# Forward step of a recurrent attention kernel: mask products, a V cast, two postponed projections and a copy are reordered

## The chip, the core and the metric

The kernel runs on one core of a Trainium2 chip. Its engines work in parallel, each through its own instructions in order: TensorE (PE, matrix products; PEld is its loading of weights), VectorE (DVE), ScalarE (ACT), GpSimd (POOL) and SyncE (SP), which here only issues DMAs. PE writes to PSUM, the others copy from there to SBUF. Sixteen DMA engines move data between SBUF and the chip's memory and within SBUF; SP's DMAs go out on one hardware queue, POOL's on a software queue. The metric is the device time of one execution in microseconds (us). Kernels are compared by the median of several executions; a profile is one further execution.

## The reference

It is one training step (forward and gradients) of a layer of recurrent attention with a small memory, followed by a SwiGLU layer. The change is in the forward of the attention alone:

```python
mem = mem0                                   # 8 rows
for s in range(n_seg):                       # 64 segments of 32 rows, D = 448
    xs = x[:, s * seg_len:(s + 1) * seg_len, :]
    h = jnp.concatenate([mem, xs], axis=1)   # 40 rows
    q = jnp.einsum('btd,dhe->bhte', h, Wq)   # 16 heads of 256
    k = jnp.einsum('btd,dhe->bhte', h, Wk)
    v = jnp.einsum('btd,dhe->bhte', h, Wv)
    scores = jnp.einsum('bhqe,bhke->bhqk', q, k) * scale
    scores = jnp.where(mask[None, None], scores, -1000000000.0)
    p = softmax(scores)
    o = jnp.einsum('bhqk,bhke->bhqe', p, v)
    o = jnp.einsum('bhte,hed->btd', o, Wo)
    mem = o[:, :M, :]                        # the next segment needs these 8 rows
    outs.append(o[:, M:, :])
```

The eight output rows that become the next segment's memory make the segments a chain.

## The kernel before

The program has five stages one after another: the load of inputs and weights with the first layer norm, the forward chain over 64 segments, the SwiGLU layer with its gradients, the backward chain over the segments, and the weight gradients. Within an engine the order of the instructions is the order in which the Python code calls them (a manual schedule); waits between engines follow from the tiles that are read and written. DMAs on SP's queue take eight completion semaphores in turn, so that a DMA is issued only when the one eight before it has landed.

**One step** (forward_chain, the loop over s; t, r = divmod(s, 4)) works on 32 of a segment's 40 rows: the memory's 8 rows and 24 of its own. The other 8 rows of each segment depend on no memory, so they are handled for four segments at once, in pieces between the steps ("postponed" work, below).

1. K, then Q is projected (proj, L471), each in two halves of 512 columns. The four row groups of PE work at once, so that a projection lies in PSUM as four groups of 32 partitions. DVE and ACT cast the halves to Kev and Qev.
2. tr_half (L485) turns them by products with a unit matrix, four blocks of 128x128 per half; DVE and ACT copy them into kT and qT. POOL puts the postponed rows of kB and qB into the same tiles (L719, L720).
3. The first half of V is projected (L479); the scores of eight heads of each half are accumulated into two PSUM tiles s_ps (L516); then the second half of V.
4. Softmax of each half: maximum and difference on DVE (L759, L761), the exponential on ACT (L763), sum, reciprocal and product on DVE (L770, L772, L773). The mask is not added there: mask_mm (L498) has put it into s_ps beforehand by a product of a unit matrix and a mask tile, two products for each half (partitions 0 to 39 and 64 to 103).
5. The casts of V (Vev) must be moved to other partitions to form V_sb: v_shift (L667, L437), of the second half two groups by DMA on SP (D_) and two by DVE (V). v_b_rows (L663) adds the postponed rows of V by four DMAs on SP.
6. P is turned by PE (p_turn, L783), copied by p_ev into PT, and multiplied with V_sb (L816), first for one half of the heads, then for the other. The outputs oA and oB are evacuated by DVE and ACT.
7. The output projection (wo_mm, L600) leaves four partial sums of each token on four partition groups. They are copied to part (L434), transposed back by two products (turn, L524), and added by gsum (L529) into hA, the next step's memory rows. This ends the chain of a step.

K, Q and P are also stored for the backward stage: KtokA, QtokA (L766, L767) and Vtok (L802) by SP, P_all (L799) by POOL.

**Postponed pieces.** In the steps r = 1, 2, 3 of a tile t, the K, Q and V rows of the next tile that need no memory are projected (b_units, "k", "q", "v"); in r = 0 the output projection of the previous tile's such rows (o_units). Each unit is cut into pieces that the step calls at fixed places: u1 and its cast e1 after the softmax, u2 between P's two turnings, u3 (8 products of 512 columns) between the two halves of the product with V, its cast e3 after gsum. One step later (`late`) ut turns the cast rows by eight products (L583) between the output projection and turn, and one more step later (`late2`) et copies them on ACT into kB or qB. So K's rows are turned in the step r = 2 and Q's in r = 3, and both are needed in the next r = 0.

Of the kernel before, what the change touches and what calls it, by code (L numbers as in the profile page):

```python
# [10 lines left out]
BF16 = mybir.dt.bfloat16  # L11
# [4 lines left out]
P = 128  # L16
# [166 lines left out]
def run_all(k: _K):  # L183
# [89 lines left out]
    with tc.tile_pool(name="wfwd", bufs=1) as wf, \  # L273
# [14 lines left out]
        nc.gpsimd.affine_select(out=maskf[:], in_=maskf[:], compare_op=ALU.is_ge, fill=-1e9 / k.scale,  # L288
                                base=0, pattern=[[-1, L]], channel_multiplier=1)
        nc.gpsimd.memset(maskf[0:M, :], 0.0)  # L290
        maskr = wf.tile([L, H // 2 * L], BF16)
        for hh in range(H // 2):
            nc.vector.tensor_copy(out=maskr[:, hh * L:(hh + 1) * L], in_=maskf[:])
        k.part = wf.tile([P, DP], FP32, name="part")
        k.partB = wf.tile([P, DP], FP32, name="partB")
        nc.vector.memset(k.part[:], 0.0)
# [110 lines left out]
def forward_chain(k: _K, hA, NWIN, Wq_sb, Wk_sb, Wv_sb, Wo_sb, maskr, work, stage, ff):  # L407
# [17 lines left out]
    def ps1(dtype=FP32):  # L425
        if dtype == FP32:
            return k.pspool.tile([P, 512], FP32, tag="ps", name="psf")
        return k.pspool.tile([P, 1024], BF16, tag="ps", name="psh")

    def V(out, in_):  # L430
        nc.vector.tensor_copy(out=out, in_=in_)

    def A(out, in_):
        nc.scalar.copy(out=out, in_=in_)  # L434
# [47 lines left out]
    def tr_half(ev, half):  # L482
        pt = ps1(BF16)
        for j in range(4):
            nc.tensor.transpose(pt[:, j * P:(j + 1) * P], ev[:, half * HB + j * P:half * HB + (j + 1) * P], ident[:, :])  # L485
        return pt[:, 0:HB].rearrange("p (j g t) -> p j g t", j=4, g=G)

    def fm_view(dst, half, t0, t1):
        return dst[:].rearrange("p (g j) n -> p j g n", g=G)[:, 4 * half:4 * half + 4, :, t0:t1]
# [5 lines left out]
    S_v = [x[0:NR, 0:HQ * L].rearrange("p (h n) -> p h n", n=L) for x in S_ps]  # L495

    def mask_mm(half):
        for gg in range(2):  # L498
            nc.tensor.matmul(S_ps[half][QB * gg:QB * gg + L, 0:HQ * L], lhsT=ident[0:L, 0:L], rhs=maskr[:, 0:HQ * L],
                             start=True, stop=False, skip_group_check=True)  # L500

    def hpos(hh):
        return (hh // 4) * 2 + hh % 2
# [34 lines left out]

    tiles = {}

    def b_units(t, which):
        W_sb = {"k": Wk_sb, "q": Wq_sb, "v": Wv_sb}[which]
        T = tiles[t]
        st = {}

        def stat(kc):
            return T.hB[0:DB, kc, :, :]

        def mm(ps, half, kcs=range(4)):
            if which == "v":  # L550
                proj_v(ps, stat, half, kcs)
            else:
                proj(ps, W_sb, stat, half, kcs)

        def u1():
            st["p0"] = ps1(FP32)
            mm(st["p0"], 0)

        def e1():
            tg = "bevv" if which == "v" else "bev"  # L560
            st["ev"] = stage.tile([P, GF], BF16, name=tg, tag=tg, bufs=2)
            A(st["ev"][:, 0:HB], st["p0"][:, :])

        def u2():
            st["p1"] = ps1(FP32)
            mm(st["p1"], 1, range(0, 2))

        def u3():
            mm(st["p1"], 1, range(2, 4))

        def e3():
            V(st["ev"][:, HB:GF], st["p1"][:, :])
            if which == "v":
                T.vB = st["ev"]
            else:
                nc.gpsimd.dma_start(out=dr["KtokB" if which == "k" else "QtokB"][t], in_=st["ev"][:])

        def ut():
            if which == "v":
                return  # L580
            pt = ps1(BF16)
            for j in range(NJ):
                nc.tensor.transpose(pt[:, j * P:(j + 1) * P], st["ev"][:, j * P:(j + 1) * P], ident[:, :])  # L583
            st["pt"] = [pt[:, half * HB:(half + 1) * HB].rearrange("p (j g t) -> p j g t", j=4, g=G) for half in range(2)]

        def et():
            if which == "v":
                return
            dst = stage.tile([P, MC, SEG], BF16, name=which + "B", tag=which + "B", bufs=2)
            for half in range(2):  # L590
                A(fm_view(dst, half, 0, SEG), st["pt"][half])
            setattr(T, which + "B", dst)
        return dict(u1=u1, e1=e1, u2=u2, u3=u3, e3=e3, ut=ut, et=et)

    partB = k.partB

# [6 lines left out]
    def o_units(t):  # L603
        T = tiles[t]
        st = {}

        def mm(i0, i1):
            for i in range(i0, i1):
                for c in range(4 * i, 4 * i + 4):
                    wo_mm(st["pO"], T.oB[:, c, :], c, c % 2, c < 2, c >= MC - 2)  # L610

        def u1():
            st["pO"] = ps1(FP32)
            mm(0, 4)

        def e1():
            pass

        def u2():
            mm(4, 6)  # L620

        def u3():
            mm(6, 8)

        def e3():
            A(partB[:, 0:2 * DB], st["pO"][:, 0:2 * DB])

        def ut():
            st["y"] = turn(partB)

        def et():
            for kc in range(KC):
                gsum(T.aT[0:DB, kc, :].rearrange("p (r j) -> p r j", r=4)[:, :, XA:SEG],
                     st["y"][:, kc, :, :].rearrange("p (r i) g -> p r i g", r=4))
        return dict(u1=u1, e1=e1, u2=u2, u3=u3, e3=e3, ut=ut, et=et)

    def none_units():
        def f():
            pass
        return dict(u1=f, e1=f, u2=f, u3=f, e3=f, ut=f, et=f)  # L640

    def out_pe(t):
        T = tiles[t]
# [25 lines left out]
    def v_shift(V_sb, Vev, half, gs, eng):  # L669
        for g in gs:  # L670
            gg, g2 = divmod(g, 2)
            o = V_sb[QB * gg:QB * gg + SEG, g2 * GF + half * HB:g2 * GF + (half + 1) * HB]
            eng(o, Vev[32 * g:32 * g + 32, half * HB:(half + 1) * HB])
# [5 lines left out]
    pend = []  # L679
    for w in "kqv":  # L680
        u = b_units(0, w)
        for n in ("u1", "e1", "u2", "u3", "e3", "ut", "et"):
            u[n]()
    V_sb = work.tile([P, 2 * GF], BF16, name="V_sb", bufs=1)
    nc.gpsimd.memset(V_sb[:], 0.0)
# [1 line left out]
    for i in range(2):  # L687
# [1 line left out]
        nc.gpsimd.memset(Ps[i][:], 0.0)  # L689
        PTs.append(work.tile([P, 2, 4, 2 * L], BF16, name=f"PT{i}", bufs=1))  # L690
        nc.gpsimd.memset(PTs[i][:], 0.0)
    mask_mm(0)
    mask_mm(1)
    late = none_units()
    late2 = none_units()

    for s in range(NSEG):
# [40 lines left out]
        V(fm_view(kT, 0, 0, SEG), tr_half(Kev, 0))  # L738
        A(fm_view(kT, 1, 0, SEG), tr_half(Kev, 1))
        V(fm_view(qT, 0, 0, SEG), tr_half(Qev, 0))  # L740
        V(fm_view(qT, 1, 0, SEG), tr_half(Qev, 1))
        if s == NSEG - 1:
            ff.load_first()
# [13 lines left out]
        for half in range(2):  # L757
# [3 lines left out]
            nc.vector.tensor_tensor(out=S_sb[half][0:NR], in0=S_v[half],  # L761
                                    in1=mx[half][0:NR].unsqueeze(2).to_broadcast([NR, HQ, L]), op=ALU.subtract)
            nc.scalar.activation(out=E_sb[0:NR, half], in_=S_sb[half][0:NR], func=ACT.Exp, scale=k.scale)  # L763
        A(Vev[:, HB:GF], pv1[:, :])
        v_shift(V_sb, Vev, 1, (0, 1), D_)
        nc.sync.dma_start(out=dr["KtokA"][s], in_=Kev[:])  # L766
        nc.sync.dma_start(out=dr["QtokA"][s], in_=Qev[:])  # L767
        for half in range(2):
# [3 lines left out]
            nc.vector.reciprocal(out=rs[half][0:NR], in_=ssum[half][0:NR])  # L772
            nc.vector.tensor_tensor(out=hsel(P_sb, half), in0=hview(E_sb[0:NR, half]),  # L773
                                    in1=hview(rs[half][0:NR].unsqueeze(2).to_broadcast([NR, HQ, L])), op=ALU.mult)
        v_shift(V_sb, Vev, 1, (2, 3), V)
        cur["u1"]()
        cur["e1"]()
        PT = PTs[s % 2]
        ppt = [ps1(BF16), ps1(BF16)]

# [4 lines left out]
        def p_ev(half, e, eng):  # L785
            eng(PT[QB * e:QB * e + L, half, :, e * L:(e + 1) * L].rearrange("p (g a) n -> p g a n", g=2),
                ppt[half][QB * e:QB * e + L, 0:2 * P].rearrange("p (a g n) -> p g a n", a=2, g=2)[:, :, :, 0:L])

        if s + 1 < NSEG:
            mask_mm(0)  # L790
            mask_mm(1)
        p_turn(0)
        p_ev(0, 0, A)
        p_ev(0, 1, A)
        cur["u2"]()
        p_turn(1)
        p_ev(1, 0, A)
# [2 lines left out]

        for gg in range(2):
            nc.sync.dma_start(out=dr["Vtok"][s, gg], in_=V_sb[QB * gg:QB * gg + 48, :])  # L802

        oAv = T.oA[:].rearrange("p (g j) n -> p g j n", g=G)
        oBv = T.oB[:].rearrange("p (g j) n -> p g j n", g=G)
        obs = []
        for half in range(2):
            if half == 1:
                cur["u3"]()
            for gg in range(2):  # L810
                po = ps1()
                pw = po[:, 0:8 * L].rearrange("p (a e c n) -> p a e c n", a=2, e=2, c=DC)
                for i in range(2):
                    for dc in range(DC):
                        c0 = gg * GF + half * HB + i * Dh + dc * P
                        nc.tensor.matmul(pw[:, i, :, dc, :], lhsT=V_sb[0:NR, c0:c0 + P],  # L816
                                         rhs=PT[0:NR, half, 2 * gg + i, :].rearrange("p (e n) -> p e n", e=2),
                                         start=True, stop=True)
                pov = po[:, 0:8 * L].rearrange("p (g j n) -> p g j n", g=2, j=4)
                eng = V if gg == 0 else A  # L820
                eng(oAv[:, 2 * gg:2 * gg + 2, 4 * half:4 * half + 4, r * SEG:(r + 1) * SEG], pov[:, :, :, 0:SEG])
                obs.append((eng, oBv[:, 2 * gg:2 * gg + 2, 4 * half:4 * half + 4, r * M:(r + 1) * M], pov[:, :, :, SEG:L]))
# [6 lines left out]
        for i in range(MC):  # L829
            c = order[i]  # L830
            wo_mm(pO, T.oA[:, c, r * SEG:(r + 1) * SEG], c, i % 2, i < 2, i >= MC - 2)
        A(part[:, 0:2 * DB], pO[:, 0:2 * DB])
        late["ut"]()
        if r == 0 and t + 1 < NT:
            xl = xl_next
            ppx = prep_pe(xl)
# [1006 lines left out]
```

## Time and profile before

| | us |
|---|---|
| runs, median of 3 | 3031.98 (3018.99 to 3051.59) |
| profiled execution | 3044.81, its span 3043.0 |

Sums of stretches of the profiled execution (busy us):

| stretch, us | what | PE | PEld | DVE | ACT | POOL | clock |
|---|---|---|---|---|---|---|---|
| 0 to 66.8 | loads, first rows | 14.59 | 5.84 | 22.04 | 8.53 | 10.91 | 0.78 |
| 66.8 to 975 | forward chain | 857.83 | 497.37 | 532.69 | 422.48 | 212.22 | 0.99 |
| 975 to 1345 | SwiGLU and its gradients | 341.97 | 179.97 | 255.79 | 204.63 | 78.08 | 0.96 |
| 1345 to 2350 | backward chain | 906.40 | 515.85 | 563.06 | 452.34 | 245.38 | 0.97 |
| 2350 to 3043 | weight gradients | 654.95 | 331.13 | 128.32 | 76.33 | 190.66 | 0.98 |

Groups of the forward chain that the change touches (mean duration of one):

| line | what | count | ns |
|---|---|---|---|
| L499 PE | mask product, 40x160 | 256 | 242 (median) |
| L583 PE | turning of postponed K, Q, 128x128 | 256 | 219 (median) |
| L434 ACT | cast of V, 128x512 | 124 | 576 |
| L434 ACT | copy into kB, qB, 128x512 | 60 | 589 |
| L434 ACT | copy of the sums, part, 128x224 | 64 | 345 |
| L431 DVE | shift of V, 32x512 | 124 | 287 |
| L437 POOL | shift of V, 32x512 | 124 | 603 |

A row of the profile gives the line of the source (often that of a helper), the engine, the operation, the tiles out<-in, the sizes and the count. Matmuls are pipelined and the profile's ends of them are modelled, so their durations overlap: what one costs is read from the distance of its start to the next start. A number in brackets is the time for which the engine was idle before, with what released it.

### The profile page before, as it was taken

The numbers are of one execution on the slowest core, as the hardware profiler recorded it, in microseconds if no ns is written. First come the engines' busy times: TensorE is split into PE (matmuls) and PEld (weight loads), VectorE is DVE, ScalarE is ACT, GpSimd is POOL, SyncE is SP. The second block draws the span as 40 slices with busy tenths as digits, with TensorE's granted clock in tenths as the row PEclk, the third lists the DMA queues.
The fourth block names the chain that finished last, engine by engine and source line by source line (L and its number), as shares of the span: only waits on it lengthen the run. The fifth ranks groups of instructions, "written<-read, shape, count | busy, mean of one in ns | idle before, by whom it ended". The sixth has DMA issues, their size and how long they took to land.

```text
span 3043.0 us, 105017 instructions
## 1 busy us (share of the span) xinstructions
PE 2775.7 (91%) x44548; PEld 1530.2 (50%) x44584; DVE 1501.9 (49%) x3931; ACT 1164.3 (38%) x3087; POOL 737.2 (24%) x1388
## 2 busy tenths in 40 slices
PE   3999999999998799986999999999997999998989
PEld 1555555555554355543555555555554454444544
DVE  3555655565555577763556655656553112111211
ACT  1444444444443456652444544544442011110100
POOL 1222222222222122221222222222222223322232
PEclk7999999999999899997999999999999999999999
DMA  9343444434444763358655665665576999999995
GB/s 252 113 129 122 129 125 126 128 123 129 129 125 141 205 157 119 123 151 178 176 144 146 183 158 150 181 160 142 149 194 227 287 211 213 194 207 188 188 199 119
DMA packets 626771, 496.14 MB, mean 163 GB/s; under 512 B 487168, under 2 KB 538960, under 8 KB 616768
## 3 DMA queue, kind: packets, MB, share of 16 engines
q1 hardware_dynamic: 577920, 297.58, 44.3%
q0 software_dynamic: 48384, 191.85, 19.5%
q8 instruction: 352, 5.77, 0.8%
q14 instruction: 115, 0.94, 0.1%
HBM read 137.63 MB, written 222.08 MB: 118 GB/s over the span
## 4 chain that ended last, share of the span: by engine, by line
PE 71%; DMA 8%; DVE 7%; issue 6%; SPq 3%; ACT 3%; POOL 1%; another core or an unknown queue 0%; POOLq 0%; ACTq 0%; DVEq 0%
PE psf L1689 12%; PE psf L1218 9%; PE psf L471 9%; PE psf L1191 4%; PE psf L600 4%; DMA V_sb<-Vev 3%; PE psf L479 3%; PE psf L1494 3%; PE psf L1674 3%; PE psf L996 3%; PE psh L485 2%; PE psf L1702 2%; PE psf L1079 2%; DMA wall<-in_A_Wv_dram 2%; PE pob L1218 2%
## 5 line engine op out<-in xcount | busy, mean ns | idle before, releaser
L1689 PE MATMUL psf<-wall,H_all 128*128 128x512 bf16 x1404 | 322.1, 382 | 17.2 <-DMA wall<-dQA 11.7
L471 PE MATMUL psf<-wall,hA 112*32 112x512 bf16 x4096 | 233.4, 380 | 17.0 <-DVE hA L529 15.2
L1689 PEld LDWEIGHTS <-H_all 128*128 128x128 bf16 x1440 | 139.8, 98 | 183.2 <-issue 27.3
L1601 DVE CAST resc<-psf 128x512 bf16<-128x512 f32 (+1 forms) x58 | 39.0, 673 | 322.9 <-PE psf L1689 288.8
L471 PEld LDWEIGHTS <-hA 112*32 112x32 bf16 x4096 | 103.5, 97 | 129.8 <-DVE hA L529 31.3
L1599 ACT CAST resc<-psf 128x512 bf16<-128x512 f32 (+1 forms) x54 | 31.0, 573 | 334.4 <-PE psf L1689 297.0
L1545 POOL COPY dmem<-dA 128x32 bf16<-128x32 bf16 x63 | 13.2, 210 | 558.6 <-DVE dA L1230 558.6
L437 POOL COPY V_sb<-Vev 32x512 bf16<-32x512 bf16 x128 | 77.2, 603 | 275.1 <-ACT Vev L434 271.3
L1182 DVE COPY partC<-psf 128x224 f32<-128x224 f32 x64 | 25.0, 391 | 230.6 <-ACT partC L1185 230.6
L1191 PE MATMUL psf<-wall,dA 128*32 128x512 bf16 x2048 | 122.4, 381 | 13.0 <-DVE dA L1230 13.0
L1674 PE MATMUL psf<-dOut_all,wall 128*128 128x448 bf16 x640 | 127.1, 358 | 7.6 <-DMA wall<-OTA 7.6
L479 PE MATMUL psf<-wall,hA 112*32 112x512 bf16 x2048 | 134.0, 382 | 0.0
L1674 PEld LDWEIGHTS <-wall 128*128 128x128 bf16 x864 | 84.5, 99 | 95.9 <-issue 14.3
L1218 PE MATMUL psf<-wall,dkA 128*32 128x448 bf16 x2048 | 113.8, 364 | 18.6 <-DMA wall<-in_A_Wk_dram 13.1
L1218 PE MATMUL psf<-wall,dqA 128*32 128x448 bf16 x2048 | 113.2, 362 | 14.9 <-DMA wall<-in_A_Wq_dram 10.6
L1182 DVE COPY dO_sb<-dOev 32x512 bf16<-32x512 bf16 x256 | 121.2, 474 | 7.0
L1218 PE MATMUL psf<-wall,dvA 128*32 128x448 bf16 x2048 | 122.2, 358 | 0.4
L600 PE MATMUL psf<-wall,oA 128*32 128x224 bf16 x4096 | 116.7, 269 | 0.0
L1218 PE MATMUL pob<-wall 128*32 128x448 bf16 x1536 | 108.1, 358 | 1.7 <-issue 1.7
L1185 ACT CAST dOev<-psf 128x512 bf16<-128x512 f32 x64 | 37.5, 585 | 183.2 <-PE psf L1191 182.0
L1185 ACT CAST wall<-psf 128x64 bf16<-128x64 f32 x512 | 106.7, 247 | 0.0
L471 PE MATMUL psf<-wall,hB 112*32 112x512 bf16 x1024 | 75.6, 397 | 30.1 <-DMA wall<-in_A_Wk_dram 18.6
(284 smaller groups left out, 5792.5 us busy)
## 6 DMA issues: line engine op xcount, KB each, us to landing
Vtok<-V_sb SPq DMA_DIRECT2D x128, 192.0 KB
KtokA<-Kev SPq DMA_DIRECT2D x64, 256.0 KB
QtokA<-Qev SPq DMA_DIRECT2D x64, 256.0 KB
OTA<-oA POOLq DMA_DIRECT2D x16, 1024.0 KB, 6.0
Q_sb<-QtokA SPq DMA_DIRECT2D x128, 128.0 KB
K_sb<-KtokA SPq DMA_DIRECT2D x128, 128.0 KB
dVA<-dvA POOLq DMA_DIRECT2D x16, 1024.0 KB, 5.1
dKA<-dkA POOLq DMA_DIRECT2D x16, 1024.0 KB, 7.3
```

The costliest lines, as they stand in the source:

```text
L437: nc.gpsimd.tensor_copy(out=out, in_=in_)
L471: nc.tensor.matmul(ps[32 * g:32 * g + 32, :], lhsT=stat(kc), rhs=W_sb[0:DB, kc, c0:c0 + HB], start=(kc == 0), stop=(kc == KC - 1))
L479: nc.tensor.matmul(ps[32 * g:32 * g + 32, :].rearrange("t (y d) -> t y d", y=2), lhsT=stat(kc), rhs=wv[:, x, :, half, e, :], start=(kc == ...
L600: nc.tensor.matmul(ps[32 * g:32 * g + 32, 0:2 * DB], lhsT=x, rhs=Wo_sb[:, c, a * 2 * DB:(a + 1) * 2 * DB], start=first, stop=last)
L996: nc.tensor.matmul(out[b][:, 0:BW], lhsT=xT[:, kc, :], rhs=Wx[:, kc, f0:f0 + BW], start=(kc == 0), stop=False)
L1182: nc.vector.tensor_copy(out=out, in_=in_)
L1185: nc.scalar.copy(out=out, in_=in_)
L1191: nc.tensor.matmul(ps[32 * g:32 * g + 32, :], lhsT=stat(kc), rhs=WoT_sb[:, kc, c0:c0 + HB], start=(kc == 0), stop=(kc == KC - 1))
L1218: nc.tensor.matmul(pO[32 * g:32 * g + 32, 0:D], lhsT=ch(c), rhs=WT[:, c, :], start=(first and i < 4), stop=(last and i >= MC - 4), skip_gr ...
L1494: nc.tensor.matmul(po[:, n * L:(n + 1) * L], lhsT=lhs[b:b + L, lc:lc + P], rhs=rhs[b:b + L, hh, 0:L], start=True, stop=True)
L1674: nc.tensor.matmul(ps[:, 0:D], lhsT=stat[:, i, c * P:(c + 1) * P], rhs=Y[:, i, 0:D], start=(i == 0), stop=(i == kts - 1))
L1689: nc.tensor.matmul(ps[:, 0:N], lhsT=Hx[:, i, dc * P:(dc + 1) * P], rhs=X[:, i, b * N:(b + 1) * N], start=(i == 0), stop=(i == kts - 1))
```

## The change

Six edits in the forward, and the tiles that they need:

- **Mask.** A lhsT of 104 columns (ident2: a unit matrix at columns 0 to 39 and again at 64 to 103) lets one product write both partition groups of a half: two mask products a step instead of four. They are called between Q's two turnings of the same step, no longer before P's turning for the next step.
- **V cast.** The second half of V is cast on ACT after the first exponential, ahead of the second; it was cast after both. Of its shifts, group 2 goes from DVE to POOL; group 3 stays on DVE.
- **e1** is called after the first two copies of PT, no longer before P's turning.
- **Postponed K and Q** are turned by dt: four DMA transposes on SP, from SBUF to SBUF, one for each group of 32 rows, called behind the two stores of Vtok in the step in which ut was. The eight products and two ACT copies of each unit go.
- **u3** in the steps r = 2 and 3 is called behind the output projection, where ut was; in r = 0 and 1 it stays.
- **Sums.** part is copied half by ACT and half by DVE.

```diff
+        ident2 = wf.tile([L, P // 2 + L], BF16, name="ident2")
+        nc.vector.memset(ident2[:], 0.0)
+        for i in range(2):
+            nc.vector.tensor_copy(out=ident2[:, i * P // 2:i * P // 2 + L], in_=ident[0:L, 0:L])
...
     def mask_mm(half):
-        for gg in range(2):
-            nc.tensor.matmul(S_ps[half][QB * gg:QB * gg + L, 0:HQ * L], lhsT=ident[0:L, 0:L], rhs=maskr[:, 0:HQ * L],
-                             start=True, stop=False, skip_group_check=True)
+        nc.tensor.matmul(S_ps[half][0:NR, 0:HQ * L], lhsT=k.ident2[:, :], rhs=maskr[:, :],
+                         start=True, stop=False, skip_group_check=True)
...
-        def ut():
...
-        def et():
+        def dt():
             if which == "v":
                 return
             dst = stage.tile([P, MC, SEG], BF16, name=which + "B", tag=which + "B", bufs=2)
-            for half in range(2):
-                A(fm_view(dst, half, 0, SEG), st["pt"][half])
+            for g in range(G):
+                nc.sync.dma_start_transpose(out=dst[:, g * NJ:(g + 1) * NJ, :], in_=st["ev"][32 * g:32 * g + 32, :])
             setattr(T, which + "B", dst)
...
         V(fm_view(qT, 0, 0, SEG), tr_half(Qev, 0))
+        mask_mm(0)
+        mask_mm(1)
         V(fm_view(qT, 1, 0, SEG), tr_half(Qev, 1))
...
             nc.scalar.activation(out=E_sb[0:NR, half], in_=S_sb[half][0:NR], func=ACT.Exp, scale=k.scale)
-        A(Vev[:, HB:GF], pv1[:, :])
+            if half == 0:
+                A(Vev[:, HB:GF], pv1[:, :])
...
-        v_shift(V_sb, Vev, 1, (2, 3), V)
+        v_shift(V_sb, Vev, 1, (3,), V)
+        v_shift(V_sb, Vev, 1, (2,), G_)
         cur["u1"]()
-        cur["e1"]()
...
-        if s + 1 < NSEG:
-            mask_mm(0)
-            mask_mm(1)
         p_turn(0)
         p_ev(0, 0, A)
         p_ev(0, 1, A)
+        cur["e1"]()
         cur["u2"]()
...
             nc.sync.dma_start(out=dr["Vtok"][s, gg], in_=V_sb[QB * gg:QB * gg + 48, :])
+        late["dt"]()
...
-            if half == 1:
+            if half == 1 and r < 2:
                 cur["u3"]()
...
-        A(part[:, 0:2 * DB], pO[:, 0:2 * DB])
+        A(part[:, 0:DB], pO[:, 0:DB])
+        V(part[:, DB:2 * DB], pO[:, DB:2 * DB])
         late["ut"]()
+        if r >= 2:
+            cur["u3"]()
```

In the prologue, dt takes the place of ut and et for tile 0.

## The prediction, made before the changed kernel ran

> **What bounds the kernel now.** I read the page's summary and slices first, then the sums by stretches, then the waits of the forward stage, then one forward step in order of time. Everything that the change touches lies in the forward stage (0 to 975 us); the rest of the span stays as it is.
>
> Sums of the stretch 100 to 960 us (length; busy us of TensorE's matmuls, of its weight loads, of DVE, ACT, POOL; granted clock; DMA share; GB/s):
>
> ```profile
> 100.00:960.00 860.00, 815.69 (x16768) 473.12 (x16762) 507.38 (x1598) 403.28 (x1075) 202.71 (x436) 0.99 0.40 126
> ```
>
> TensorE looks 95% busy, its weight loads 55%. The 63 rows of hA<-psf (the sum that ends a step) start 14.0 to 16.5 us apart, mean 14.38. The four kinds of step (r = s mod 4) share the floor of 14.0; over it lie 22.9 us in all, mostly in about 20 steps of up to 0.96 us each. The costliest matmul group that waits, and one step of kind r=3 in order of time (start, length, engine, line):
>
> ```profile
> L816 PE MATMUL psf<-PT,V_sb 104*128 104x80 bf16 x992 | 72.7, 203 | 30.0 <-DMA V_sb<-Vev 22.9 <-ACT PT L434 3.3 <-PE psh L783 0.8
> ```
>
> ```profile
> 521.52 0.74 PE L516 MATMUL s_ps<-kT,qT 128*40 128x40 bf16 x32
> ...
> 522.19 1.05 PE L479 MATMUL psf<-wall,hA 112*32 112x512 bf16 x16
> ...
> 523.35 0.34 ACT L763 ACTIVATE E_sb<-S_sb 104x160 f32<-104x160 f32 x1 [0.25 <-DVE S_sb L761]
> 523.58 0.18 DVE L772 RECIPROCAL rs<-ssum 104x4 f32<-104x4 f32 x1
> 523.60 0.57 ACT L434 CAST Vev<-psf 128x512 bf16<-128x512 f32 x1
> 523.79 0.33 DVE L773 TENSOR_TENSOR P_sb<-E_sb,rs 104x160 bf16<-104x160 f32 x1
> ...
> 524.03 0.32 PE L499 MATMUL s_ps<-maskr,ident 40*40 40x160 bf16 x4
> 524.04 0.31 DVE L770 TENSOR_REDUCE ssum<-E_sb 104x4 f32<-104x160 f32 x1
> ...
> 524.60 0.32 DVE L773 TENSOR_TENSOR P_sb<-E_sb,rs 104x160 bf16<-104x160 f32 x1
> 524.63 0.97 ACT L434 COPY PT<-psh 40x160 bf16<-40x160 bf16 x3
> ...
> 525.02 0.26 PE L783 MATMUL psh<-ident,P_sb 104*128 104x104 bf16 x2
> ...
> 526.26 0.73 PE L816 MATMUL psf<-PT,V_sb 104*128 104x80 bf16 x8
> ```
>
> To be seen: from the scores (521.52) to the second turning of P (525.02) two chains run side by side and end together. TensorE does products one after another; DVE does ten softmax operations without a gap, its last ending at 524.92, and P's turning starts 0.10 later. So TensorE is full, but work taken off it there uncovers the DVE chain.
>
> One rule reads the same rows otherwise. The Trainium skill (Perfetto Trace Analysis, Identifying the Most-Contended Engine) says that matmul busy time misjudges TensorE and that weight-load time is to be used; by that, 55% means that removed TensorE work is worth nothing, by the 95% row it is worth its whole time. No run here shows yet which.
>
> **The change, part by part.** Times are of the step above, whose hA sum ends at 515.78.
>
> *Masks (L498).* Four products of 160 columns between 524.03 and the turning at 524.28 (0.25 us) become two, moved between Q's turnings. At the old place the turning then waits for the first P (523.79 + 0.33, and 0.10 as at 525.02: 524.22), so 0.06 is won, on a piece that ends in the second P anyway. At the new place TensorE waits for ACT's cast of Q (ends 520.15) about 0.12 us, and two products take about 0.13. I take 0. Bounds: -0.12 a step (two products fewer, TensorE alone deciding: -7 us over 63 steps), +0.13 (the wait does not hide them: +8).
>
> *V cast between the exponentials.* The cast needs the second V projection, whose last group starts at 522.85; the first cast starts 0.56 after its own last group. So 523.40 instead of 523.60, ending 523.97 instead of 524.17: the V shifts by DMA start 0.20 earlier. But the second exponential is behind it: 523.95 to 524.29 instead of 523.35 to 523.69. The second sum starts at 524.32 instead of 524.04, and with it P, its turning and the first P·V product are 0.2 to 0.3 late in every step. On r=0 and 1 the later products follow in a row: +0.23 at the start of the second half's P·V, of which about 0.05 vanishes in a wait for the last V shift that the floor already holds. +0.18 in 31 steps: +5.6 us. On r=2 and 3 the third projection piece (u3, 8 products, 0.55 from start to start) no longer stands before the second half; that half then waits for PT: turning 525.30, ACT's copy, then DVE's, which queues behind ACT's (L434 to 525.60, L431 at 525.64 now), gives 526.3 against 526.26. About +0.02 in 32 steps: +0.6.
>
> *The late V shifts.* In a floor step the four shifts (L667) are issued by 9.55 after the step's start and their last packet ends at 10.49; P_all's packets start at 10.55 (DMA packet records). In the late steps an issue slips by 0.1 to 0.8 us, the packets run into P_all's and end at 10.6 to 11.35. With shifts 0.20 earlier and P_all 0.28 later (it waits for the second P) a slip of up to 0.5 stays clear. Of the 22.9 us over the floor I ascribe 15 to such steps: -15 us; bounds 0 (they slip into something else) and -19. One V copy goes from DVE (0.60 for two) to POOL (0.60 each), which is free from 523.7 to 525.2 apart from it: 0; without that cover P_all would be late, which harms nobody.
>
> *Sums in two halves.* Both copies read one PSUM tile. The backward stage has this form already (start, length, engine):
>
> ```profile
> 1523.24 0.34 ACT L1185 COPY partC<-psf 128x224 f32<-128x224 f32 x1 [7.34 <-PE psf L1218]
> 1523.62 0.39 DVE L1182 COPY partC<-psf 128x224 f32<-128x224 f32 x1 [7.70 <-ACT partC L1185]
> ```
>
> DVE starts when ACT has ended. Here (ACT 345 ns for 224 columns, 225 for 64, hence about 255 for 112; DVE 391 and 214, about 273) the second half is there 0.56 after the start, and its transpose begins at 0.61; now it begins at 0.55, behind the first. +0.06 a step, +3.8 us. If they ran at once: -0.08, -5 us.
>
> *K and Q turned by DMA, u3 postponed.* On r=2 and 3 TensorE loses eight transposes (0.57, 528.57 to 529.14) behind the output projection. They cover the copy of the sums; u3 now covers it with the same length. 0 for TensorE; ACT's two copies (1.07) at the step's start lie in idle time. If TensorE alone decided: -0.45 in 30 steps, -13.5. On SP four transposes are issued behind Vtok (ends 513.50 in the r=2 step, 528.40 here), ahead of the next step's four V rows (L663, 2.7 to 3.8 us) and its V shifts (from 522.37). No row has a transpose out of SBUF; the nearest is from HBM:
>
> ```profile
> L1335 SPq DMA_TRANSPOSE vT<-Vtok x128: 1237/1293/2318, 1356.7 to 2282.7; - x128
> ```
>
> 1.24 us for 48 tiles of 16x128, and 1.23 for the 64 tiles of wall<-dVA; the 392 of w_gate took 6.21, so 0.015 a tile above 64. Ours have 16: between 0.5 (that slope carried down) and 1.3; I take 1.0. Four at 1.24 end at 518.5, the V rows at 521.2 to 522.2: the shifts are not late. On the step from r=3 to r=0 POOL's copy of qB (0.40) must be done when the scores start, 5.74 into the step, at 535.57. The transposes end at 532.4 (at 1.0) or 533.4, and land 1.1 later (vT's packets) or up to 4.4 where 1 MB stores run beside, as OTA does from 530.5. That is 533.5 to 537 against 535.1: 0 to 2 us in 15 steps, 0 to +28. Most land ahead of OTA's packets: +1.
>
> The Trainium skill (Advanced Engine Details and Errata, X-Bar Transpose (TRN2)) has transposes as fast as regular DMAs. The rows disagree for the issue, 1.24 against 0.42 for the same 192 KB as Vtok; by the page the four would take 1.7 and this term would be 0.
>
> *Prologue.* qB's last transpose shares a semaphore with Wo's load (eight in turn), whose packets end near 72.3. Issue and landing (1.24 + 1.2) and the copy give 75.2; the scores now start at 73.54. +2 us; bounds 0 and +6, as V's first rows on POOL queue behind that copy.
>
> Sum: 0 + 5.6 + 0.6 - 15 + 3.8 + 1 + 2 = -2 us.
>
> **The rivals.** *TensorE alone decides* (for it: 95% busy; against: the turning that starts 0.10 after P). Then -7, -13.5, -15 and +2 give -34 us: 2998.
>
> *SP's queue becomes the bound*, slower. A transpose out of SBUF might be issued in smaller pieces. SP has about 6.1 us between Vtok and the V rows that must precede the shifts, so this decides from 1.5 us a transpose on; each further us puts 4 us on 30 steps, +120. At 1.8 us it is +36: 3068; at 2.5, +120: 3152. For: nothing in the trace turns out of SBUF. Against: all three HBM rows.
>
> *The exponential's delay without the gain*: the shifts stay as late as they are. 63 steps at 0.28, +3.8 and +3: +24, 3056.
>
> *The change is not what it says*: the order on each engine shows the two mask products, the cast between the exponentials and 128 transposes on SP as described, and DVE's half waiting for ACT. Only the halves do less than their name.
>
> **How the numbers follow.** The profiled execution took 3044.81 us (span 3043.0), the runs' median is 3031.98 (3018.99 to 3051.59); I apply the sum to the median: 3030. A measurement of this kernel tells about 1% from no change, 30 us. Chances: forecast 0.58 (2% of a step either way stays within 1%), TensorE alone 0.22, SP 0.13, no gain from the shifts 0.07 (within 1%, but with a late qB added half of it is slower). So faster 0.22, same 0.62, slower 0.16. The range reaches to TensorE's case and to the bounds of masks, halves and qB: 2995 to 3062; SP's case is left out, with the faster edge of TensorE's.
>
> **What would show it.** Right: second P·V half no earlier than 10.4 us into r=2 and 3 steps; the second exponential some 0.6 us after where it was; DVE's part copy starting at ACT's end; L816's waits for V_sb<-Vev well below 22.9 us; steps at a floor near 14.1 to 14.3 with few at 14.9. Wrong: a floor below 13.8 (TensorE decided), transposes on SP above 1.5 us each, or the scores of r=0 steps waiting for POOL.

## The result, and the profile after

| | before | changed |
|---|---|---|
| runs, median (lowest to highest), us | 3030.61 (3018.99 to 3051.59) | 3114.03 (3105.92 to 3119.08) |
| profiled execution, its span, us | 3044.81, 3043.0 | 3119.08, 3117.0 |

The ratio is 1.0265 (95% interval 1.0203 to 1.0327): slower. All of it lies in the forward chain (the rest of the profiled execution is 11 us shorter than before; two profiles of one kernel, e6 and e10 below, differ by 9 there). From here on a step is counted from the end of one sum hA<-psf to the end of the next; there are 62 of them, and their sum is compared. The columns r=0 to r=3 hold 15 steps each: the first two steps are in the sum of all 62 alone. The floor is the median of the fastest third of a kind of step.

| steps, us | r=0 | r=1 | r=2 | r=3 | all 62 | at half clock |
|---|---|---|---|---|---|---|
| before | 214.9 | 215.3 | 217.4 | 215.3 | 891.2 | 13.7 |
| changed | 265.1 | 217.9 | 219.0 | 244.9 | 976.1 | 102.4 |

84.9 us are lost, 50.2 of them in r=0 and 29.6 in r=3: the steps behind the two quads of DMA transposes (kB at the end of r=2, qB at the end of r=3). r=1 and r=2 cost 0.1 to 0.2 a step.

The sums of the stretch shown for before, now:

```profile
100.00:960.00 860.00, 767.48 (x14936) 440.22 (x14928) 472.09 (x1452) 334.77 (x922) 221.60 (x451) 0.95 0.45 123
```

TensorE is 89% busy in place of 95%, and its granted clock has gone from 0.99 to 0.95: it waits, and it runs slower besides. P·V in the same stretch:

```profile
L814 PE MATMUL psf<-PT,V_sb 104*128 104x80 bf16 x864 | 59.2, 206 | 32.4 <-DMA V_sb<-Vev 22.9 <-DVE PT L436 3.2 <-ACT PT L439 1.9
```

The wait for the V shifts is 22.9 us as before, with 864 products recorded in place of 992, so nothing of it went. What is new is a wait for qB. The view of that tile (of an issue: ns least/median/longest; of a wait: us, times):

```profile
L590 SPq DMA_TRANSPOSE qB<-bev x64: 1181/1300/3509, 65.7 to 1012.5; - x64
...
its engine sat idle before it (us, times) until:
  DMA qB<-bev: 81.8, 16
who waited for it (us, times):
  POOL qT L716: 81.8, 16
  PEld L520: 52.3, 15
  PE s_ps L520: 44.9, 15
```

In 15 steps the scores wait for POOL's copy, and that for qB (8.2 of the 44.9 us in the very first step, ahead of the 62). One such step (r=0, begins at 507.47) in order of time (start, length):

```profile
505.20 9.00 SPq L590 DMA_TRANSPOSE qB<-bev x4
...
508.14 0.58 POOL L854 DMA_DIRECT2D OTA<-oA  x1 [0.33 <-issue]
...
512.46 1.05 PE L484 MATMUL psf<-wall,hA 112*32 112x512 bf16 x16
...
514.37 3.14 SPq L661 DMA_DIRECT2D V_sb<-bevv  x4
516.95 0.40 POOL L716 COPY qT<-qB 128x256 bf16<-128x256 bf16 x1 [6.74 <-DMA qB<-bev]
...
517.40 0.93 PE L520 MATMUL s_ps<-kT,qT 128*40 128x40 bf16 x32 [3.89 <-POOL qT L716]
517.61 1.18 SPq L665 DMA_DIRECT2D V_sb<-Vev  x2
...
518.26 1.90 PE L484 MATMUL psf<-wall,hA 112*32 112x512 bf16 x16
```

The four issues hold SP for 9.00 us, and TensorE stands still for 3.89. The V rows and first V shifts come late behind them on SP. And the same 16 products of L484 take 1.05 us before the wait and 1.90 after it. The windows of these microseconds show why (columns as above; the third from the end is the granted clock):

```profile
512.00:514.00 2.00, 1.51 (x22) 0.59 (x21) 0.87 (x3) 0.80 (x2) 0.00 (x0) 1.00 0.77 215
514.00:516.00 2.00, 0.00 (x0) 0.00 (x0) 0.00 (x0) 0.20 (x1) 0.00 (x0) 1.00 0.42 85
516.00:518.00 2.00, 0.60 (x27) 0.60 (x28) 0.00 (x0) 0.00 (x0) 1.00 (x3) 0.56 0.09 16
518.00:520.00 2.00, 2.00 (x35) 0.88 (x33) 1.81 (x7) 0.34 (x1) 0.56 (x1) 0.50 0.19 41
520.00:522.00 2.00, 2.00 (x42) 1.31 (x38) 0.95 (x5) 0.84 (x3) 0.61 (x1) 0.50 0.01 2
522.00:524.00 2.00, 2.00 (x46) 1.33 (x41) 0.80 (x3) 1.21 (x4) 0.56 (x1) 0.74 0.57 178
```

After the wait the clock is 0.50, from 516.22 to 523.05. The steps have 24 such stretches (3 before), each 3.41 or 6.83 us long. In r=0, 11 of the 14 waits of 1.4 to 4.2 us are followed by one. Such a wait is paid twice: once standing still, and again at half speed.

### The profile page after: what moved, and what is told of

It reads as the page before. It is cut to its first block, busy times and chain, and to the rows that moved or that the text cites. A ratio compares the mean times of both kernels' runs of the same rounds, so it can differ in the third digit from the quotient of the medians.

```text
span 3117.0 us, 104530 instructions
## 1 busy us (share of the span) xinstructions
PE 2795.7 (90%) x44164; PEld 1540.9 (49%) x44200; DVE 1514.5 (49%) x3930; ACT 1127.4 (36%) x3023; POOL 781.8 (25%) x1452
## 4 chain that ended last, share of the span: by engine, by line
PE 65%; DMA 9%; DVE 9%; SPq 7%; issue 6%; ACT 2%; POOL 1%; POOLq 0%; ACTq 0%; DVEq 0%
PE psf L1690 12%; PE psf L1219 8%; PE psf L476 6%; PE psf L1192 4%; PE psf L599 4%; PE psf L1495 3%; PE psf L1675 3%; PE psf L484 3%; DMA qB<-bev 3%; PE psf L997 3%; SPq L590 2%; DMA V_sb<-Vev 2%; PE psf L1703 2%; PE psf L1080 2%; PE psh L490 2%
## 5 line engine op out<-in xcount | busy, mean ns | idle before, releaser
L476 PE MATMUL psf<-wall,hA 112*32 112x512 bf16 x4096 | 233.4, 380 | 17.0 <-DVE hA L533 15.2
L442 POOL COPY V_sb<-Vev 32x512 bf16<-32x512 bf16 x192 | 119.2, 621 | 270.9 <-ACT Vev L439 267.2
L484 PE MATMUL psf<-wall,hA 112*32 112x512 bf16 x2048 | 143.1, 402 | 0.0
L599 PE MATMUL psf<-wall,oA 128*32 128x224 bf16 x4096 | 128.3, 286 | 0.0
L1219 PE MATMUL psf<-wall,dkA 128*32 128x448 bf16 x2048 | 111.9, 361 | 13.7 <-DMA wall<-in_A_Wk_dram 12.5
L814 PE MATMUL psf<-PT,V_sb 104*128 104x80 bf16 x1024 | 71.2, 208 | 44.0 <-DMA V_sb<-Vev 33.2
L599 PEld LDWEIGHTS <-oA 128*32 128x32 bf16 x4096 | 105.6, 106 | 9.8
L439 ACT CAST Vev<-psf 128x512 bf16<-128x512 f32 x128 | 75.1, 587 | 93.5 <-PE psf L484 80.1
```

Source lines behind the costliest of these rows:

```text
L442: nc.gpsimd.tensor_copy(out=out, in_=in_)
L476: nc.tensor.matmul(ps[32 * g:32 * g + 32, :], lhsT=stat(kc), rhs=W_sb[0:DB, kc, c0:c0 + HB], start=(kc == 0), stop=(kc == KC - 1))
L484: nc.tensor.matmul(ps[32 * g:32 * g + 32, :].rearrange("t (y d) -> t y d", y=2), lhsT=stat(kc), rhs=wv[:, x, :, half, e, :], start=(kc == ...
L599: nc.tensor.matmul(ps[32 * g:32 * g + 32, 0:2 * DB], lhsT=x, rhs=Wo_sb[:, c, a * 2 * DB:(a + 1) * 2 * DB], start=first, stop=last)
L1219: nc.tensor.matmul(pO[32 * g:32 * g + 32, 0:D], lhsT=ch(c), rhs=WT[:, c, :], start=(first and i < 4), stop=(last and i >= MC - 4), skip_gr ...
```

## The experiments

Floors, sums of the 62 steps and the time over the floors (of 60 steps, without the first two) are from each run's one trace; ratios are against runs of the kernel before on the same chip.

**The transposes alone, and everything but them.** The first edit puts only dt and the postponed u3 into the kernel before (e2):

```diff
-        def ut():
...
-        def et():
...
+        def dt():
...
+            for g in range(G):
+                nc.sync.dma_start_transpose(out=dst[:, g * NJ:(g + 1) * NJ, :], in_=st["ev"][32 * g:32 * g + 32, :])
...
+        late["dt"]()
```

> The kernel before with only K and Q turned by DMA and u3 postponed. Theory A: r=0 steps about 265 us in sum (215 before), r=3 steps about 245 (215), r=1 and r=2 within 3 us of before, total 2.3 to 3.0% above before. Theory B: the transposes alone cost less than half of it, total at most 1.3% above.

Ratio 1.0259 (1.0213 to 1.0305). Steps 964.2: r=0 255.5, r=3 245.8, r=1 and 2 218.7 and 216.1. The tile view has the same waits:

```profile
L586 SPq DMA_TRANSPOSE qB<-bev x64: 1181/1370/3414, 63.9 to 999.9; - x64
...
  PEld L516: 45.1, 14
  PE s_ps L516: 38.2, 14
```

The second is the changed kernel with ut, et and u3 as before (e1):

> The changed kernel with K and Q turned by TensorE again and the third projection piece (u3) back at its old place; mask products, V cast, V shifts and sums as changed. Theory A (the transposes on SP and what waits behind and for them are the whole loss): the 62 steps, 891.2 us before and 976.1 after, take 886 to 903; the floors stay 0.1 to 0.25 above 14.0 from the other edits; the half-clock windows of the forward stage go from 24 back to about 3; total within 0.7% of before. Theory B (the second exponential behind the V cast, or the copy in halves, makes shifts and products late, and the transposes only add to it): steps sum to more than 930 and total 1.2% or more above before.

Ratio 1.0025 (0.9997 to 1.0053), steps 899.8, 13.7 us at half clock. 73.0 us from the transposes and 8.6 from the rest make 81.6 of the 84.9: the parts add up, and theory B falls.

**One transpose per unit (e3).**

```diff
-            dst = stage.tile([P, MC, SEG], BF16, name=which + "B", tag=which + "B", bufs=2)
-            for g in range(G):
-                nc.sync.dma_start_transpose(out=dst[:, g * NJ:(g + 1) * NJ, :], in_=st["ev"][32 * g:32 * g + 32, :])
+            dst = stage.tile([P, NJ, P], BF16, name=which + "B", tag=which + "B", bufs=2)
+            nc.sync.dma_start_transpose(out=dst[:], in_=st["ev"][:, :])
```

> The changed kernel with one transpose of all 128 rows per unit (64 tiles) in place of four of 32 rows (16 tiles each); POOL's copies read it through another view. The same bytes and the same 1024 packets of 256 B. Theory A1 (what counts is SP's time for issuing, four times a fixed 1.25 us and more): one issue takes 1.2 to 2.5 us, r=3 steps go back to 215 to 219, qB lands ahead of the scores in most r=0 steps (215 to 230), total within 1% of before. Theory A2 (what counts is the transfer itself: issue time goes by tiles or by packets, landing is as late): the one issue takes 5 us or more, or qB lands as late; r=0 stays at 245 or more, total 1.5% or more above before.

Ratio 1.0026 (1.0002 to 1.0049): the loss by the transposes is gone (r=0 217.4, r=3 220.1) with the bytes and packets unchanged.

```profile
L589 SPq DMA_TRANSPOSE qB<-bev x16: 1569/2269/2758, 61.5 to 934.5; - x16
...
  PE s_ps L520: 4.5, 1
```

64 tiles in one issue take 2.27 us, four issues of 16 took 7.00 in the mean; the scores wait once (in the first step) and not 15 times. One issue with four times the tiles takes 1.57 in place of 1.18 us at the least and 2.27 in place of 1.30 in the middle: its price goes mostly by the instruction, and less by the tile. That is theory A1.

**Where the landing is lost (e5).** OTA's store (1 MB) leaves POOL 0.7 us into r=0. Here it goes behind P_all of that step, and the four transposes stay:

```diff
+    def store_o(t):
+        nc.gpsimd.dma_start(out=dr["OTA"][t], in_=tiles[t].oA[:].rearrange("p c n -> p (c n)"))
+        nc.gpsimd.dma_start(out=dr["OTB"][t], in_=tiles[t].oB[:].rearrange("p c n -> p (c n)"))
...
         nc.gpsimd.dma_start(out=dr["P_all"][s], in_=P_sb[0:NR].rearrange("p h n -> p (h n)"))
+        if r == 0 and t > 0:
+            store_o(t - 1)
...
-        if r == 3:
-            nc.gpsimd.dma_start(out=dr["OTA"][t], in_=T.oA[:].rearrange("p c n -> p (c n)"))
-            nc.gpsimd.dma_start(out=dr["OTB"][t], in_=T.oB[:].rearrange("p c n -> p (c n)"))
```

> The changed kernel with the stores of OTA and OTB (1 MB and 256 KB, issued by POOL 0.7 and 1.2 us into the r=0 step) issued behind P_all of that step instead; the four transposes stay. Theory A3 (the last transposes of qB are issued beside or behind that store and lie behind its packets in the DMA engines): issues of the r=3 quad fall to 1.25 to 1.5 us each, the last packet of qB comes 0.5 to 1 us after the fourth issue's end (1.3 to 4.2 now), r=0 steps go from 265 to 218 to 238, r=3 steps stay at 240 to 250, total 25 to 50 us below the changed kernel. Rival (SP's issue time alone is what is waited for): r=0 steps stay at 250 or more.

Ratio 1.0155 (1.009 to 1.0221); r=0 226.9, r=3 239.1. The r=0 step that begins at 484.45:

```profile
482.16 5.98 SPq L590 DMA_TRANSPOSE qB<-bev x4
...
488.31 2.77 SPq L661 DMA_DIRECT2D V_sb<-bevv  x4
489.44 0.40 POOL L720 COPY qT<-qB 128x256 bf16<-128x256 bf16 x1 [3.38 <-DMA qB<-bev]
490.43 0.74 PE L520 MATMUL s_ps<-kT,qT 128*40 128x40 bf16 x32
```

The copy of qB begins 1.30 us after the last issue (2.75 in the step shown above), and the scores wait for nothing (in the whole run 3 times). By the packets, qB's last one ends 0.4 to 1.8 us after the last issue, with the store beside it 1.3 to 4.2. So 38 of the 50 us in r=0 come from the store beside the last transposes. It acts in two ways: without it a quad of qB takes 6.12 in place of 7.00 in the mean, and from the last issue to POOL's copy there are 1.8 in place of 4.0. e3's one issue ends before the store leaves, and avoids it as well. r=3 keeps its loss: there the V rows and shifts are late behind kB's quad on SP. In the changed kernel the rows' last issue ends 5.6 to 9.0 into those steps (mostly 4.5 in e1), and the first shift by DMA leaves at 6.75 to 9.3 (6.75 in e1).

**The clock (e4).** Eight useless products are put ahead of the scores of r=0:

```diff
+        if r == 0 and t > 0:
+            fill = ps1()
+            for i in range(8):
+                nc.tensor.matmul(fill[:, :], lhsT=ident[0:DB, :], rhs=Wk_sb[0:DB, i % KC, 0:512], start=True, stop=True)
         scores(qT, kT, 0)
```

> The changed kernel with eight useless products of 512 columns (about 1.7 us) on TensorE ahead of the scores of r=0 steps, where it waits 1 to 4.3 us for qB. Theory C (over half of the loss is the clock, halved for 3.41 us or twice that after such a wait: 25.9 us lost in r=0 steps by the granted clock): with the wait filled the half-clock windows of r=0 fall to a third or less, r=0 steps go from 265 to 245 to 255, total 10 to 20 us below the changed kernel. Theory D (the clock is not bound to these waits): r=0 stays at 262 or more, up to 290 where the products are not hidden.

What the clock takes from r=0 (its missing share, summed over the steps' time) falls from 25.9 to 3.8 us, r=0 from 265.1 to 254.4. The ratio, 1.0236 (1.019 to 1.0281), cannot be told from the changed kernel's. So the low clock is bound to the waits; as its price, 11 us of r=0 are shown with work added that is useless and not all hidden. That the clock is over half of the loss, as theory C has it, is not shown. How the 85 us divide between standing and half speed stays open beyond that (102.4 us at half speed are worth at most 51, against 7 before).

**The other edits, one by one.** Only the mask products (e9), only the V cast (e6, and again e10), only the sums in halves (e7), each in the kernel before, as in the diff above. Of e6, e7 and e9 there is a profile alone and no ratio:

> The kernel before with only the mask products changed: one of 104 rows per half, between Q's two turnings. By the prediction the floors stay at 14.0 (bounds 13.88 and 14.13). By the rows of the runs so far (the scores start 5.97 into a step wherever these products stand there, 5.73 elsewhere): scores at 5.97 and floors at 14.22 to 14.28 in all four kinds, nothing won at the old place.

> The kernel before with only the V cast moved between the two exponentials. By the prediction: floors +0.18 on r=0 and 1 (14.18), +0.02 on r=2 and 3 (14.02 to 14.08), V shifts (second pair) issued 0.20 earlier than 8.41. If the cast does not come earlier at all because its own product ends late, the shifts move by 0.1 or less and nothing is won from the steps above the floor.

> The kernel before with only the V cast between the exponentials, timed. Its look had floors of 13.80 to 13.84 on r=0, 1 and 2 and 14.0 on r=3 (14.0 before) with the second pair of V shifts issued at 8.11 in place of 8.41, but 33 us over the floors (21 before). If that excess was chance, 0.994 to 0.998 of before; if earlier shifts only collide with other transfers, 0.998 to 1.003.

> The kernel before with only the copy of the sums split between ACT and DVE. By the prediction: floors 14.06 to 14.10 in all four kinds, DVE's half starting where ACT's ends. Rival (the halves run at once): 13.9 to 13.95.

| floors | r=0 | r=1 | r=2 | r=3 | all 62 | over the floors |
|---|---|---|---|---|---|---|
| before | 14.01 | 14.03 | 14.02 | 14.03 | 891.2 | 21 |
| masks (e9) | 14.25 | 14.25 | 14.26 | 14.25 | 909.1 | 25 |
| cast (e10) | 13.79 | 13.84 | 13.84 | 13.88 | 897.0 | 39 |
| halves (e7) | 14.12 | 14.12 | 14.11 | 14.13 | 895.8 | 20 |

*Masks* cost 0.23 a step. TensorE's order in e9:

```profile
459.76 0.39 PE L490 MATMUL psh<-ident,Qev 128*128 128x128 bf16 x4
...
460.07 0.34 PE L503 MATMUL s_ps<-maskr,ident 40*104 40x160 bf16 x2
...
460.35 0.40 PE L490 MATMUL psh<-ident,Qev 128*128 128x128 bf16 x4
```

From start to start the two take 0.28 us; the scores begin 5.97 into the step (5.73 before). The *cast* takes 0.2 off the floor: the second pair of V shifts is issued 8.11 into the step in place of 8.41 and its last packet ends at 10.20 in place of 10.49. But the time over the floors rises, and the timed ratio is 1.0033 (1.001 to 1.0056). e6, the same kernel as e10, has floors of 13.80 to 13.84 and 14.00 on r=3, steps of 893.7 and 33 us over the floors: two profiles of one kernel differ by 3 us in the sum and by 0.13 in one floor. *Halves* cost 0.10; DVE's half waits for ACT's:

```profile
L431 DVE COPY part<-psf 128x112 f32<-128x112 f32 x64 | 17.6, 275 | 117.4 <-ACT part L434 117.4
```

**Combinations.** One transpose per unit, with cast and halves as before (e8); cast and one transpose per unit, masks and halves as before (e11); cast and two mask products at their old place (e12):

> The changed kernel with one transpose per unit, and the V cast and the copy of the sums as before; what stays of the change is the mask products, one V copy on POOL, K and Q turned by DMA and u3 postponed. If cast and halves carry the 0.12 to 0.19 by which the floors rose, the floors are back at 14.00 to 14.03 and the total is 0.992 to 1.000 of before. If the masks between Q's turnings or the postponed u3 carry it, the floors stay at 14.1 or more. If TensorE alone decided, the floors of r=2 and 3 would be 13.5 to 13.6 and the total below 0.992.

> The kernel before with the V cast between the exponentials, one transpose per unit and u3 postponed; masks and the copy of the sums as before. If SP's 2.2 us per unit cost nothing and the cast's 0.2 a step stays: floors 13.75 to 13.85 in all kinds, 0.992 to 0.998 of before. If the transposes' packets push V shifts late: excess of 35 us or more over the floors, 0.998 to 1.004.

> The kernel before with the V cast between the exponentials and the two mask products of 104 rows in place of four of 40, at their old place ahead of P's turning. If the products' form sets nothing there (P's turning waits for DVE): floors as with the cast alone, 13.80 to 13.84 and 14.0. If two products of 104 rows cost more than four of 40 in two column groups (0.24 against 0.25 between Q's turnings): the same; if they push P's turning, floors 0.05 to 0.1 higher.

e8: 1.003 (1.0002 to 1.0058), floors 14.25 to 14.28, so the masks' cost stays. e11: 0.9981 (0.9954 to 1.0008), floors 13.72 to 13.84, 41 us over them. e12: 0.9995 (0.9966 to 1.0023), floors 13.79 to 13.91: the form of the products sets nothing at the old place; their new place is what costs.

**What lies over the floors.** In e13 the second half's V shifts leave the DMA queue:

```diff
-        v_shift(V_sb, Vev, 1, (0, 1), D_)
+        v_shift(V_sb, Vev, 1, (0,), A)
+        v_shift(V_sb, Vev, 1, (1, 2), G_)
...
-        v_shift(V_sb, Vev, 1, (2, 3), V)
+        v_shift(V_sb, Vev, 1, (3,), V)
```

> The kernel before with the V cast between the exponentials and the second half's V shifts made by engines alone (ACT one, POOL two, DVE one) in place of two by DMA and two on DVE; the first piece's cast of the postponed projections stands behind ACT's copies of P. If the late shifts by DMA make the floor and the steps above it: floors 13.6 to 13.8, time over the floors below 12 us (21 before, 33 to 39 with the cast), few or no half-clock windows, total 0.985 to 0.993 of before. If the steps above the floor come from elsewhere: 20 us or more stays over the floors, total 0.993 to 1.000.

e14 adds one transpose per unit, u3 postponed and e12's mask products:

> As e13, with one transpose per unit for K and Q, u3 postponed, and the two mask products of 104 rows at their old place. If nothing waits on SP any more: floors of r=2 and 3 0 to 0.3 below e13's (TensorE has eight transposes less there), total 0.980 to 0.992 of before. If the V rows and the first shifts behind the transposes still come late: r=0 and r=3 above e13's by 0.3 a step or more.

e13: 0.9996 (0.9962 to 1.003), floors 14.09 to 14.14, 8 us over them. P·V no longer waits for shifts:

```profile
L818 PE MATMUL psf<-PT,V_sb 104*128 104x80 bf16 x976 | 62.3, 202 | 3.9 <-DMA V_sb<-Vev 2.9 <-ACT PT L434 0.4 <-PE psf L818 0.2
```

So most of the late steps do come from the V shifts by DMA, but the floor rose by 0.1. e14: 0.9933 (0.9896 to 0.997), 4 us over floors of 14.09 and 14.14 on r=0 and 1 and 13.9 on r=2 and 3. The floor is held by a row of DVE, here in e14 (r=1):

```profile
534.61 0.32 DVE L774 TENSOR_TENSOR P_sb<-E_sb,rs 104x160 bf16<-104x160 f32 x1
534.75 1.32 POOL L442 COPY V_sb<-Vev 32x512 bf16<-32x512 bf16 x2 [0.27 <-ACT Vev L439]
...
535.52 0.72 DVE L774 TENSOR_TENSOR P_sb<-E_sb,rs 104x160 bf16<-104x160 f32 x1
```

The second P takes 0.72 while POOL's last copy (to 536.07) runs; the first, which had begun before POOL's first copy did, takes 0.32. e15 gives that copy (group 2) back to DVE:

> e14 with one of POOL's two late V copies made by DVE behind the second P, as before the change. If POOL's copy beside DVE's second P is what stretches it from 0.32 to 0.72: second P 0.32 again, its turning 0.3 to 0.4 earlier, floors 13.75 to 13.9 on r=0 and 1 and 13.5 to 13.7 on r=2 and 3, total 0.980 to 0.990 of before. If the chain is held elsewhere: floors stay at 14.1 and 13.9, total 0.990 to 0.997.

```profile
529.33 0.32 DVE L774 TENSOR_TENSOR P_sb<-E_sb,rs 104x160 bf16<-104x160 f32 x1
...
529.68 0.60 DVE L436 COPY V_sb<-Vev 32x512 bf16<-32x512 bf16 x2
```

0.32 again, floors 13.70 to 13.81, steps 863.8. The ratio is 0.9898 (0.9863 to 0.9933): 1% faster than before. e14 and e15 are the two versions whose interval lies wholly below 1. On r=2 and 3 the floors are 13.80 and not below 13.7. In 19 of the 24 steps at that floor the second half of P·V waits 0.4 to 0.5 us for DVE's copy of PT, here in r=3:

```profile
544.76 0.45 PE L818 MATMUL psf<-PT,V_sb 104*128 104x80 bf16 x8 [0.47 <-DVE PT L436]
```

There, with u3 no longer ahead of that half, the way from the second P to this copy holds the step and not TensorE. No run shortens it.

## Why the prediction was wrong

The forecast was 3030 (2995 to 3062); the time is 3114. Step by step:

- **K and Q turned by DMA: +1, measured +73** (e2). This is the step that failed, in four places. *The issue*: "I take 1.0" from a slope carried down. 16 tiles take at least 1.18, where 48 take at least 1.24 in the row shown: few tiles save little, and the bound of 1.3 had that row as its end when it should have been the likeliest value. Of 120 issues 65 stay below 1.4 us; the other 55 take up to 3.51, and during them the 16 DMA engines are busy 76% of the time in the mean, against 54% during the 65. A quad takes 6.54 (kB) and 7.00 (qB) in the mean, 1.69 for each of its four. *The V rows*: "the shifts are not late" had the rows issued 5.4 to 6.4 into r=3; they are issued by 5.6 to 9.0, and the first V shift leaves at 7.9 in the middle, 6.75 in e1. With the half clock after its waits this makes the loss of r=3, which e3 takes back. *The landing*: "most land ahead of OTA's packets" followed from 1.0; at 1.7 the last ones are behind them (e5). *The clock*: the prediction had a wait cost its length; here the products after it ran at half clock as well. The Trainium skill (TensorE: Matmul & The Clock Gate, Part 1: The HAM clock gate) has a clock that is either full or half, decided over free-running windows of 3.41 us. The trace agrees: 0.50 or 1.00, in stretches of 3.41 or 6.83 us. The prediction did not weigh this. How the 73 us divide among the four is not shown.
- **The rival on SP's queue** named place and threshold (1.5 us each) rightly, but priced SP's time alone: at 1.69 it gives +23. The landing and the clock were left out of it.
- **The Trainium skill's transposes as fast as regular DMAs** (Advanced Engine Details and Errata, X-Bar Transpose (TRN2)): at the issue the trace disagrees out of SBUF too, 2.27 for the 256 KB of e3's single one, against 0.53 for KtokA's store of the same size.
- **Masks: 0 (bounds -7 and +8), measured +0.23 a step, +14** (e9; the sum of its steps is 18 longer). "Two products take about 0.13" was half of the truth (0.28 start to start), and the wait for ACT's cast hides almost nothing of them: they start 0.31 after the first of Q's first four transposes, where before the change Q's second four started 0.35 after it. In e9 these start at 0.59. Why the mask products do not start earlier in that wait stays open.
- **V cast: +6.2 and the late shifts: -15.** Both signs were wrong (e10): the floor falls by 0.2, so the landing of the shifts held it, not the second P, which is 0.11 later though its exponential is 0.42 later; DVE catches up. The terms that were mis-sized are the "+0.23 at the start of the second half's P·V" (in floor steps of r=1 10.48 into the step before and 10.53 in e10, so 0.05) and the "about 0.05" of waiting that vanishes: that half's last product starts at 10.79 in place of 10.99, so the half itself is 0.25 shorter. But the late steps do not go: a slip hits the earlier shifts as it did the later ones. That they are the shifts' was right (e13). Why SP's issues slip stays open.
- **Halves: +3.8, measured +0.10 a step, +6** (e7; the sum of its steps is 4.6 longer). The mechanism was right, the price too small.
- **These four parts together**: -5 forecast, +8.6 measured (e1). That they come so near is partly luck: the masks' miss and the cast's have opposite signs.
- **TensorE alone decides** was rightly doubted: in e2, with eight transposes less, the floor of r=2 is 14.01 (14.02 before; r=3 is late there). Once nothing waits for the shifts (e14 against e13) 0.24 of their 0.45 appear on r=2 and 3; in e14 u3 has moved as well and ACT's two copies are gone, so the 0.24 is not shown to be the transposes' alone. Neither of the two readings, worth nothing and worth the whole time, comes out.
- **Prologue: +2.** The first hA sum ends at 83.34 (83.66 before); between runs it varies from 73 to 84, so the term cannot be read.

## What to carry to other kernels

Price a DMA by its issue on its queue, per instruction and with the queue's other work behind it, and ask which large store will start before it lands; one issue for four pieces was worth 2.4% here (1.0265 against 1.0026). A new wait on a full TensorE has to be charged again for the half clock that may follow: here it did after 11 of 14 waits of 1.4 to 4.2 us. Where the floor of a loop is held by a landing, take the transfer off the queue before trimming TensorE: in e2 nothing of the removed products showed, in e14 the edit that removes them was worth 0.24 us a step.

## What was unexpected of the hardware

DVE's product of two tiles, 104x160, takes 0.72 us beside a copy on POOL and 0.32 without (e14, e15). The Trainium skill (GPSIMD Engine Reference, 1. Specifications) has the two engines share their way to SBUF, with contention for DVE instructions of two SBUF inputs; this row is such a one and agrees. The time that a V shift's issue takes on SP (0.51 to 1.93 before) was also wider than the floor steps suggested. The time over the floors goes with it, but not with it alone: in e10 the last shift's issue ends later than 9.3 us into the step in 23 of the 28 steps that lie 0.3 or more over the floor, and in 5 of the other 32.
